# A two-layer transformer kernel: VectorE's score tile chosen further ahead, row sums laid over 128 partitions, LayerNorm without negated means, two memsets dropped

## The chip, the cores and the metric

The kernel runs on one core of one Trainium2 chip. The metric is device microseconds of one execution. A few executions are taken per kernel, and each version is timed in the same rounds and on the same chip as the kernel before. The experiments ran in four such sets of rounds on different chips, where the median of the kernel before lay between 1650.24 and 1652.71 us; a difference between versions of different sets is less sure by as much. Runs of a kernel mostly agree within about 0.3%; the widest spread of one set is 0.5%. The trace of each kernel is of one profiled execution.

The engines, as the profile names them: PE is TensorE (PEld its weight loads), DVE is VectorE, ACT is ScalarE, POOL is GpSimd, SP issues most DMAs.

## The reference

Two layers, each of attention and a gated feed-forward block, both behind a LayerNorm without weights. 2,048 tokens, width 512, 32 heads of 16, feed-forward width 1,792, bfloat16 inputs.

```python
def _layernorm(x, axis=-1, eps=1e-5):
    m = jnp.mean(x, axis=axis, keepdims=True)
    v = jnp.var(x, axis=axis, keepdims=True)
    return (x - m) / jnp.sqrt(v + eps)
# A: qkv, softmax(q k^T / 4) v, output projection; 32 heads of 16
# B: (gelu(x w_gate) * (x w_up)) w_down
x = A_x
x = x + A(_layernorm(x)); x = x + B(_layernorm(x))     # the same weights in both layers
x = x + A(_layernorm(x)); x = x + B(_layernorm(x))
```

## The kernel before

The program is recorded by a scheduler that runs at build time. Each instruction is given an assumed cost in microseconds (`cost`, `us`). The scheduler plays the engines forward in assumed time, and each engine's instruction order follows from that. On the chip the order is fixed: TensorE executes its matmuls in that order and stops at the first one whose semaphore, the signal that its operand is ready, has not come; a timeline below shows it stopped for 1.1 to 1.7 us.

A score tile is 128 keys by 512 queries for one head (two halves of 256 in the last block). A slot computes two or three tiles for ScalarE, which exponentiates them in one instruction (`PT<-PS`), and perhaps one more for VectorE. VectorE makes its exponential with integer arithmetic on the float16 bits (`PI<-PS`) and three shifted copies (`PP<-PI`). That costs four PV matmuls for the tile instead of one. VectorE's tile is chosen here:

```python
    def pick(look=False):
        cap = slot_cap()
        want_d = not look and started_all() and behind() < LAG and vector_tile()  # vector_tile: VectorE not late
        ...
        a, d = [], None
        for x in cur:
            if len(a) == cap and (d is not None or not want_d):
                break
            t = x[3]                                   # tile number; t % 4 is its row group
            if want_d and d is None and d_tile(x) and (not dg["items"] or dg["uk"] == x[:3]):
                if len(a) == cap or all(y[3] % 4 != t % 4 for y in a):
                    d = x
                    continue
            if len(a) < cap:
                a.append(x)
            elif x[3] > a[-1][3] + 3 or x[:3] != a[-1][:3]:
                break
        return a, d
```

LayerNorm is bn_stats on VectorE, three small GpSimd instructions, and one instruction per 128 rows that applies it ("the normalisation" below). That last one is on VectorE for the whole first LayerNorm, and in each later LayerNorm on GpSimd for three of the four blocks of 512 tokens and on VectorE for the last (abridged):

```python
    def ln_scale(n, then, lo=0):
        ...
        job("pool", 1, [
            (lambda e: e.tensor_scalar(LNS[:, 0, lo:lo + n], var, LN_EPS, None, op0=ALU.add), ..., 0.25),
            (lambda e: e.tensor_tensor(LNS[:, 1, lo:lo + n], LNS[:, 0, lo:lo + n], CM05[:, 0:n], op=ALU.pow), ..., 0.45 + 0.16 * n),
            (lambda e: e.tensor_scalar(LNS[:, 2, lo:lo + n], mean, -1.0, None, op0=ALU.mult), ..., 0.25)], then)

    def ln_apply(i, rows, key, eng, alt, then=None, us=None, st=0):
        us = us or (1.05 if eng == "pool" else 0.46)          # the assumed cost
        job(eng, 1, [(lambda e: e.tensor_scalar(xn(i, alt), rows, LNS[:, 2, st + i:st + i + 1], LNS[:, 1, st + i:st + i + 1],
                                                op0=ALU.add, op1=ALU.mult), ..., us)], then, ported=True)
```

TensorE then transposes the normalised rows (`HT`), and the projections of the feed-forward block or of the next layer follow. The row sums of the softmax are gathered by DMA into `LT` (16 partitions by 128 per head group, 8 in the half blocks), inverted there by VectorE, written to DRAM (`rscr`) and loaded, spread, into `RB`. GpSimd multiplies that into the attention output (`AT`). Where TensorE has nothing ready, the scheduler inserts filler matmuls (`ONB` by `ZV`), which are meant to keep its clock up.

Of the kernel before, what the change touches and what calls it, by code (L numbers as in the profile page):

```python
# [14 lines left out]
AP = bass.AP  # L15
# [160 lines left out]
def _emit_fast(nc, es, x_in, wqkv, wo, wg, wu, wd, out, n_rep=2):  # L176
# [193 lines left out]
    sch.op("pool", lambda e: e.memset(OKV[:], 1.0), w=[("OKV",)])  # L370
    sch.op("pool", lambda e: e.memset(AP(VP, 16, [[NKT * H * VW, 128], [VW, NKT * H]]), 1.0), w=[("VPONE",)], cost=0.9)
    sch.op("pool", lambda e: e.memset(OKL[:], 1.0), w=[("OKL",)], cost=0.2)
    sch.op("pool", lambda e: e.memset(LT[:], 1.0), w=[("LT", i) for i in range(NG)], cost=0.2)
    sch.op("pool", lambda e: e.memset(RB[:], 0.0), w=[("RB", i) for i in range(NRB)], cost=0.9)
    dma("sp", "ldw_o", WO[:], wo.rearrange("(a p) n -> p a n", p=128), w=[("WO",)], kb=512)


# [205 lines left out]

    def ln_scale(n, then, lo=0):
        keys = [("MV", lo + i) for i in range(n)]
        mean = AP(MV, 2 * lo, [[16, 128], [2, n]])
        var = AP(MV, 2 * lo + 1, [[16, 128], [2, n]])
        job("pool", 1, [
            (lambda e: e.tensor_scalar(LNS[:, 0, lo:lo + n], var, LN_EPS, None, op0=ALU.add), keys,
             [("LNS", lo + i) for i in range(n)], 0.25),  # L590
            (lambda e: e.tensor_tensor(LNS[:, 1, lo:lo + n], LNS[:, 0, lo:lo + n], CM05[:, 0:n], op=ALU.pow),
             [("LNS", lo + i) for i in range(n)] + [("CM05",)], [("LNS", lo + i) for i in range(n)], 0.45 + 0.16 * n),
            (lambda e: e.tensor_scalar(LNS[:, 2, lo:lo + n], mean, -1.0, None, op0=ALU.mult),
             keys + [("LNS", lo + i) for i in range(n)], [("LNS", lo + i) for i in range(n)], 0.25)], then)

    def ln_check(n, lo=0):
        var = AP(MV, 2 * lo + 1, [[16, 128], [2, n]])
# [2 lines left out]

    def ln_apply(i, rows, key, eng, alt, then=None, us=None, st=0):
        us = us or (1.05 if eng == "pool" else 0.46)
        job(eng, 1, [(lambda e: e.tensor_scalar(xn(i, alt), rows, LNS[:, 2, st + i:st + i + 1], LNS[:, 1, st + i:st + i + 1],
                                                op0=ALU.add, op1=ALU.mult),
                      [key, ("LNS", st + i)], [xnkey(i, alt)], us)], then, ported=True)

    def transpose_piece(i, tt, alt=False, eng="dve", then=None):
        def fn(e, bs):
# [244 lines left out]
    def normalise(layer, qb, gs, half, h):  # L853

        n = len(gs)
        lr = 16 if h is None else 8
        np_ = lr * n
        q0, qn = (0, 512) if h is None else (256 * h, 256)
        hs = (0, 1) if h is None else (h,)
        lk = [("LT", i) for i in range(n)]  # L860
        ops = [(lambda e: e.reciprocal(LT[0:np_, :], LT[0:np_, :]), lk, lk, 0.87)]
        final = h == 1 and gs[-1] == NG - 1
        go = move_act if final else move

        def then(o):
            there = []
            checks = []
            for lim, op in ((1.0 / L_LO, ALU.is_le), (1.0 / L_HI, ALU.is_ge)):
                checks.append((lambda e, lim=lim, op=op: e.scalar_tensor_tensor(
                    OKL[0:np_, :], LT[0:np_, :], lim, OKL[0:np_, :], op0=op, op1=ALU.mult),  # L870
                    lk + [("OKL",)], [("OKL",)], 0.31))
            dve(1, checks, got(("ok", layer, qb, h, gs[-1])))

            def stored(o, i):
                there.append(i)
                if len(there) == n:
                    lt["held"] = False
                    while lt["next"]:
                        lt["next"].pop(0)()
                g = gs[i]  # L880
                rs_here.add((layer, qb, h, g))
                if (layer, qb, h, g ^ 1) in rs_here:
                    pairs_q.append(((layer, qb * NG + (g | 1), h), lambda: spread(g & ~1)))
                    next_pair()

            for i in range(n):
                g = gs[i]
                go(0, "rs%d" % i, AP(RSC, (RC(qb, h, g) * 8 + g % 2) * 512, [[2 * 512, 4], [1, qn]]),
                   LT[lr * i:lr * i + lr, :], [("LT", i)], [("RSC", RC(qb, h, g), g % 2)],
                   lambda o, i=i: stored(o, i), kb=8)  # L890

        def spread(g):
            c = g // 2
            slot = rb_free.pop(0)
            here = []
            ds = [os_of.pop((layer, qb * NG + g + k, h)) for k in range(2)]
            assert g % 2 == 0 and ds[1] == ds[0] + 1

            def landed(o):
                here.append(o)  # L900
                if len(here) == 2:
                    job("pool", 1, [(lambda e: e.tensor_tensor(AT[:, c, q0:q0 + qn], OP[:, slot, 0:qn], RB[:, slot, 0:qn],  # L902
                                                               op=ALU.mult),
                                     [("OP", slot), ("RB", slot)], [("AT", c, k) for k in hs], 0.03 + 0.00258 * qn)],
                        done)

            def done(o):
                have.update(("norm", layer, qb, h, g + k) for k in range(2))
                rb_free.append(slot)
                next_pair()  # L910

            move(0, "op%d" % slot, OP[:, slot, 0:qn],
                 OSD[ds[0] // 2, :, 0:qn],
                 [("OSD", d, j) for d in ds for j in range(4)], [("OP", slot)], landed, kb=qn / 2)
            go(0, "rb%d" % slot, RB[:, slot, 0:qn],
               AP(RSC, RC(qb, h, g) * 8 * 512, [[512, 8], [0, 16], [1, qn]]),
               [("RSC", RC(qb, h, g), k) for k in range(2)], [("RB", slot)], landed, kb=qn / 2)

        dve(1, ops, then)
# [6 lines left out]
    def evac(layer, u, part):  # L926
# [13 lines left out]
        def then(o):  # L940
            acc["free"] = True
            if part == "A":
                return
            og = list(range(NG))
            sizes = [NG - 2, 1, 1] if h == 1 else [NG - 2, 2]
            pos = g
            k, lo = 0, 0
            while pos >= lo + sizes[k]:
                lo += sizes[k]
                k += 1  # L950
            i = pos - lo
            lr = 16 if h is None else 8
            units_done[layer] += 1
            bd = block_done[layer, qb, h] = block_done.get((layer, qb, h), 0) + 1

            gone = []

            def put(o):
                gone.append(o)
                if len(gone) == 4:  # L960
                    os_free.append(s)
                    stored_os.add((layer, u, h))
                    next_pair()
                    if h != 1 or g != NG - 1:
                        gathered(o)

            def put_out(o):
                for j in range(4):
                    move(0, "os%d_%d" % (s, j), OSD[d // 2, 32 * j + 16 * (d % 2):32 * j + 16 * (d % 2) + 16, 0:qn],
                         OS[32 * j:32 * j + 16, s, 0:qn], [("OS", s)], [("OSD", d, j)], put, kb=qn / 16)  # L970
                if h == 1 and g == NG - 1:
                    gathered(o)

            def gathered(o):
                if i == sizes[k] - 1:
                    lt["held"] = True
                    normalise(layer, qb, og[lo:lo + sizes[k]], k % 2, h)

            d = (layer * NU + u + (NG if h == 1 else 0)) % NOD
            os_of[layer, u, h] = d  # L980

            def gather():
                (move_act if h == 1 and g == NG - 1 else move)(0, "lt%d" % i, LT[lr * i:lr * i + lr, :],
                     AP(OS, 16 * NOS * 512 + s * 512, [[32 * NOS * 512, 4], [1, qn]]),
                     [("OS", s)], [("LT", i)], put_out)
            if lt["held"]:
                lt["next"].append(gather)
            else:
                gather()
            if bd == NG:  # L990
                posts.append(post(layer, qb, h))
# [262 lines left out]
    def pick(look=False):  # L1254
# [4 lines left out]
        if bd is None or sch.ready("pe", w=[BK[bd]]) > now[0] + 0.02:  # L1259
            want_d = False  # L1260
        a, d = [], None
        for x in cur:
            if len(a) == cap and (d is not None or not want_d):
                break
            t = x[3]
            if want_d and d is None and d_tile(x) and (not dg["items"] or dg["uk"] == x[:3]):
                if len(a) == cap or all(y[3] % 4 != t % 4 for y in a):
                    d = x
                    continue
            if len(a) < cap:  # L1270
                a.append(x)
            elif x[3] > a[-1][3] + 3 or x[:3] != a[-1][:3]:
                break
        return a, d

    def pull():
        while len(cur) < 6 and nxt[0] < len(segs):
# [1293 lines left out]
```

## Time and profile before

Before: 1653.57 us, the median of 3 runs (1649.52 to 1655.59).

The profile page of the kernel before: first the busy time of each engine, its share of the span and its number of instructions, then two lines of the chain that ended last, by engine and by line.

```profile
PE 1559.9 (95%) x16441; PEld 521.8 (32%) x16441; DVE 1362.6 (83%) x2336; ACT 1568.5 (95%) x1351; POOL 176.6 (11%) x233
...
ACT 60%; PE 31%; DVE 6%; DMA 1%; issue 1%; POOL 1%; SPq 0%; DVEq 0%; POOLq 0%
ACT fPT L1387 57%; PE fPS L1373 9%; PE fPS L1519 8%; PE fPS L1054 7%; PE fPS L633 3%; ACT fHT L1336 2%; PE fPS L1118 2%; DVE fPI L1427 2%; DVE fPP L1467 2%; PE fPS L1539 1%; DMA fRB<-rscr 1%; ACT L1336 1%; PE fPS L700 1%; DVE fHT L1073 0%; 
```

ScalarE is the engine to watch. The chain runs through its exponential for 57% of the span, the largest share of any line. TensorE's 95% contains filler, so its share alone says little.

Groups of instructions of the kernel before, shapes apart. A line gives source line, engine, operation, output<-input, shapes and count; then busy us, mean ns of one; then idle us of the engine just before them and who ended it. Records of exponentials overlap on ScalarE: the busy times of the two groups below add up to 1,672 us, and together they cover only 1,492.5.

```profile
L1387 ACT ACTIVATE fPT<-fPS 128x1536 bf16<-128x1536 f32 x652 | 972.5, 1492 | 27.2 <-PE fPS L1373 24.4
L1387 ACT ACTIVATE fPT<-fPS 128x1024 bf16<-128x1024 f32 x655 | 699.5, 1068 | 6.5 <-PE fPS L1373 5.5
...
L603 POOL TENSOR_SCALAR fHT<-fX,fLNS 128x512 f16<-128x512 f32 x36 | 29.1, 814 | 2.1 <-PE fPS L1373 0.4 <-POOL fLNS L593 0.2
...
L593 POOL TENSOR_SCALAR fLNS<-fMV 128x2 f32<-128x2 f32 x25 | 8.1, 326 | 2.3
...
L861 DVE RECIPROCAL fLT<-fLT 96x128 f32<-96x128 f32 x7 | 6.6, 940 | 0.0
...
L603 DVE TENSOR_SCALAR fHT<-fX,fLNS 128x512 f16<-128x512 f32 x12 | 6.1, 535 | 1.8 <-POOL fLNS L593 1.8
...
L861 DVE RECIPROCAL fLT<-fLT 8x128 f32<-8x128 f32 x2 | 1.9, 936 | 0.6 <-DMA fLT<-fOS 0.6
```

Of 4,096 score tiles, 830 go to VectorE and the others to 1,307 exponentials. ScalarE is idle for 27.2 + 6.5 = 33.7 us before exponentials in all. A reciprocal takes 0.94 us, whether for 96 partitions or 8.

Who waited for whom, kernel before: us in total, times, longest us.

```profile
ACT fPT L1387 <- PE fPS L1373: 29.9, 62, 3.7
...
PE fPS L610 <- POOL fHT L603: 0.5, 1, 0.5
```

TensorE waits almost never for GpSimd's normalised rows: once, 0.5 us.

### The profile page before, as it was taken

The page shows a single profiled execution, that of the slowest core. Times are in us where ns is not written, and L with a number is a line of the kernel's source. Part 1 is how long each engine was busy: PE and PEld are TensorE (multiplying, and loading weights), DVE is VectorE, ACT ScalarE, POOL GpSimd, SP SyncE. Part 2 cuts the span into 40 slices and gives each one's busy share as a digit, 9 for nine tenths or more (in the row PEclk, how much of TensorE's full clock was granted, in tenths as well). Part 3 has the DMA queues.
Part 4 walks back from the last instruction along what each step waited for, and adds up shares of the span by engine and source line. Part 5 has one row for each costly group of instructions (what it writes and reads, how often), then busy time and mean ns, then how long its engine had stood idle before and what let it go on. Part 6 is the DMA issues. An engine that isn't in the chain of part 4 may idle for free.

```text
span 1650.3 us, 38750 instructions
## 1 busy us (share of the span) xinstructions
PE 1559.9 (95%) x16441; PEld 521.8 (32%) x16441; DVE 1362.6 (83%) x2336; ACT 1568.5 (95%) x1351; POOL 176.6 (11%) x233
## 2 busy tenths in 40 slices
PE   8999899999999999999999989999999998999998
PEld 3332222222222223332333322222222222444455
DVE  7989998879988899887743999988898879888773
ACT  6999999999999999999999999999999999899981
POOL 3420010002100210002410110100010000100000
PEclk9999999999999999999999999999999999999999
DMA  5200101123011321113123010220401123022234
GB/s 147 59 8 8 45 22 52 43 75 96 21 53 36 105 56 28 56 33 110 44 65 120 12 55 19 59 58 24 124 21 48 48 63 88 20 65 61 74 117 118
DMA packets 120962, 97.22 MB, mean 59 GB/s; under 512 B 11472, under 2 KB 103888, under 8 KB 120784
## 3 DMA queue, kind: packets, MB, share of 16 engines
q1 hardware_dynamic: 116928, 89.95, 19.1%
q0 software_dynamic: 2112, 4.19, 1.0%
q8 instruction: 133, 2.18, 0.6%
q10 hardware_dynamic: 1744, 0.53, 0.1%
q14 instruction: 45, 0.37, 0.1%
HBM read 76.81 MB, written 15.20 MB: 56 GB/s over the span
## 4 chain that ended last, share of the span: by engine, by line
ACT 60%; PE 31%; DVE 6%; DMA 1%; issue 1%; POOL 1%; SPq 0%; DVEq 0%; POOLq 0%
ACT fPT L1387 57%; PE fPS L1373 9%; PE fPS L1519 8%; PE fPS L1054 7%; PE fPS L633 3%; ACT fHT L1336 2%; PE fPS L1118 2%; DVE fPI L1427 2%; DVE fPP L1467 2%; PE fPS L1539 1%; DMA fRB<-rscr 1%; ACT L1336 1%; PE fPS L700 1%; DVE fHT L1073 0%; ACT L1387 0%
## 5 line engine op out<-in xcount | busy, mean ns | idle before, releaser
L1387 ACT ACTIVATE fPT<-fPS 128x1536 bf16<-128x1536 f32 (+1 forms) x1307 | 1492.5, 1279 | 33.7 <-PE fPS L1373 29.9
L1427 DVE TENSOR_SCALAR fPI<-fPS 128x512 int16<-128x512 f32 x830 | 564.1, 684 | 111.3 <-PE fPS L1373 105.6
L1373 PE MATMUL fPS<-fQ,fKT 32*128 32x512 f16 (+1 forms) x4608 | 528.7, 359 | 57.5 <-ACT fPT L1387 43.2
L1519 PE MATMUL fPS<-fPT,fVP 128*17 128x512 bf16 (+1 forms) x3676 | 463.1, 359 | 8.2 <-DVE fOS L937 3.8
L1467 DVE TENSOR_SCALAR fPP<-fPI 128x2048 int16<-128x2048 int16 (+3 forms) x705 | 427.0, 636 | 11.8 <-PE fPS L1519 5.6
L1519 PE MATMUL fPS<-fPP,fVD 128*17 128x512 f16 (+1 forms) x2796 | 394.1, 359 | 2.2 <-POOL fVD L713 0.9
L1373 PEld LDWEIGHTS fPS<-fQ,fKT 32*128 32x128 f16 x4608 | 142.8, 91 | 535.2 <-ACT fPT L1387 385.0
L1519 PE MATMUL fPS<-fPI,fVP 128*17 128x512 f16 (+1 forms) x932 | 256.1, 359 | 1.7 <-DVE fOS L937 1.0
L1054 PE MATMUL fPS<-fXNT,fWR 128*128 128x512 f16 (+1 forms) x952 | 219.5, 362 | 6.3 <-DVE fHT L1097 4.6
L1519 PEld LDWEIGHTS fPS<-fPT,fVP 128*17 128x17 f16 x3676 | 117.9, 88 | 151.3 <-issue 89.9
L902 POOL TENSOR_TENSOR fAT<-fOP,fRB 128x512 f16<-128x512 f32 (+1 forms) x36 | 43.7, 1214 | 1124.2 <-DMA fRB<-rscr 1124.2
L1539 PE MATMUL fPS<-fONB,fZV 128*17 128x512 f16 x1804 | 143.3, 387 | 1.7 <-POOL fQMASK L364 1.5
L1519 PEld LDWEIGHTS fPS<-fPP,fVD 128*17 128x17 f16 x2796 | 107.0, 89 | 103.4 <-issue 48.5
L1118 PE MATMUL fPS<-fWR,fHT 128*128 128x512 bf16 x428 | 118.2, 383 | 0.5 <-DVE fQ L679 0.3
L1054 PEld LDWEIGHTS fPS<-fXNT,fWR 128*128 128x128 bf16 x952 | 77.0, 97 | 111.8 <-issue 21.6
L1097 DVE TENSOR_TENSOR fHT<-fPS,fHT 128x512 bf16<-128x512 f32 x112 | 76.4, 688 | 42.5 <-PE fPS L1054 32.0
L1073 DVE CAST fHT<-fPS 128x512 bf16<-128x512 f32 x105 | 71.6, 686 | 29.4 <-PE fPS L1054 29.3
L1519 PEld LDWEIGHTS fPS<-fPI,fVP 128*17 128x17 f16 x932 | 64.0, 88 | 36.1 <-issue 19.0
L713 POOL TENSOR_SCALAR fVD<-fVP 128x544 f16<-128x544 f16 (+1 forms) x48 | 54.1, 1129 | 110.5 <-DVE fVP L721 107.8
L1539 PEld LDWEIGHTS fPS<-fONB,fZV 128*17 128x17 f16 x1804 | 42.1, 91 | 47.8 <-issue 24.4
L937 DVE COPY fOS<-fPS 128x512 f32<-128x512 f32 (+1 forms) x72 | 45.0, 625 | 13.7 <-PE fPS L1519 13.3
L679 DVE TENSOR_SCALAR fQ<-fPS,fQMASK 128x512 f16<-128x512 f32 (+1 forms) x72 | 46.1, 681 | 6.1 <-PE fPS L633 6.1
(71 smaller groups left out, 657.4 us busy)
## 6 DMA issues: line engine op xcount, KB each, us to landing
fWR<-in_B_w_up_dram SPq DMA_DIRECT2D x62, 256.0 KB, 2.9
fWR<-in_B_w_down_dram SPq DMA_DIRECT2D x58, 256.0 KB, 2.8
fWR<-in_B_w_gate_dram SPq DMA_DIRECT2D x57, 256.0 KB, 5.1
oscr<-fOS SPq DMA_DIRECT2D x224, 32.0 KB, 1.7
fOP<-oscr SPq DMA_DIRECT2D x28, 256.0 KB, 2.7
fRB<-rscr SPq DMA_DIRECT2D x28, 256.0 KB
fX<-in_A_x_dram POOLq DMA_DIRECT2D x4, 1024.0 KB, 5.8
xscr<-fX SPq DMA_DIRECT2D x16, 256.0 KB, 2.9
```

The lines of the kernel that those rows point to most:

```text
L633: ins = e.matmul(bank(bs[0])[:, 0:cols], lhsT=l, rhs=r_, start=(i == 0), stop=(i == n - 1))
L713: job("pool", 2, [(lambda e, dst=dst, src=src, ph=ph: e.tensor_scalar(dst, src, 2.0 ** (-ph / NPH), None, op0=ALU.mult), [("VP", c, k) for ...
L1054: ins = e.matmul(bank(bs[0])[:, w * qn:(w + 1) * qn], lhsT=wchunk(s, (ft + w) % 2, ck), rhs=XNT[:, ck, xs], start=(ck == 0), stop=(ck == N ...
L1073: evac_job(1, b, [(lambda e: e.tensor_copy(in_ht(ft), in_bank(b)), [BK[b]], fk, 0.6)], got(("gate", layer, qb, h, ft)))
L1097: (lambda e: e.tensor_tensor(in_ht(ft), in_bank(b), in_ht(ft), op=ALU.mult), [BK[b]] + fk, fk, 0.62)], got(("up", layer, qb, h, ft))))
L1118: ins = e.matmul(bank(b)[:, 0:D], lhsT=HT[:, ft, i * 128:(i + 1) * 128], rhs=wslot(s)[:, jj * D:(jj + 1) * D], start=(ft == 0), stop=(ft = ...
L1373: ins = e.matmul(bank(b)[:, b0:b0 + qn], lhsT=KT[32 * j:32 * j + 32, (x[1] % NG) // 2, kt * 128:(kt + 1) * 128], rhs=Q[32 * j:32 * j + 32, ...
L1387: o = sch.op("act", lambda e: e.activation(PT[:, p, 0:512 * na].rearrange("p (a b) -> p a b", a=na), PS[:, b0:b0 + na, :], ACTF.Exp, scale ...
L1427: dve(0, [(lambda e: e.tensor_scalar(PI[:, gi, 512 * r:512 * (r + 1)], bank(bd), DBIAS, 0.0, op0=ALU.add, op1=ALU.max), [BK[bd]], [("PI", ...
L1467: shifts.append((s, [(lambda e: e.tensor_scalar(PP[:, s, 0:512 * n], PI[:, gi, 0:512 * n], int(OCT) * ph // NPH, None, op0=ALU.add), [("PI ...
L1519: ins = e.matmul(PS[32 * j:32 * j + VW, ACC, 0:qn], lhsT=l, rhs=r_, start=a, stop=z, tile_position=(0, 32 * j), skip_group_check=True)
L1539: ins = e.matmul(PS[32 * j:32 * j + VW, ACC, :], lhsT=ZV[:, :], rhs=ones, start=False, stop=False, tile_position=(0, 32 * j), skip_group_c ...
```

## The change

The intent: choose VectorE's tile so that its 32-row group of the array is free and its matmul runs beside the others; invert the row sums with all 128 partitions, so that a reciprocal has 96 columns or fewer; drop the negated mean, a GpSimd instruction, by subtracting the mean directly; drop two memsets that are no longer needed.

```diff
-    sch.op("pool", lambda e: e.memset(LT[:], 1.0), w=[("LT", i) for i in range(NG)], cost=0.2)
-    sch.op("pool", lambda e: e.memset(RB[:], 0.0), w=[("RB", i) for i in range(NRB)], cost=0.9)
 ... in ln_scale
-            (lambda e: e.tensor_scalar(LNS[:, 2, lo:lo + n], mean, -1.0, None, op0=ALU.mult), ...
 ... in ln_apply
-        job(eng, 1, [(lambda e: e.tensor_scalar(xn(i, alt), rows, LNS[:, 2, st + i:st + i + 1], LNS[:, 1, st + i:st + i + 1],
-                                                op0=ALU.add, op1=ALU.mult),
+        job(eng, 1, [(lambda e: e.tensor_scalar(xn(i, alt), rows, MV[:, st + i, 0:1], LNS[:, 1, st + i:st + i + 1],
+                                                op0=ALU.subtract, op1=ALU.mult),
 ... in normalise; the DMAs to and from LT and the two checks likewise
-        ops = [(lambda e: e.reciprocal(LT[0:np_, :], LT[0:np_, :]), lk, lk, 0.87)]
+        ops = [(lambda e: e.reciprocal(LT[:, 0:nw], LT[:, 0:nw]), lk, lk, 0.07 + 0.0068 * nw)]
 ... in pick
-        for x in cur:
-            if len(a) == cap and (d is not None or not want_d):
+        spare = None
+        for k, x in enumerate(cur):
+            if len(a) == cap and (d is not None or not want_d or k >= 12):
                 break
...
-                if len(a) == cap or all(y[3] % 4 != t % 4 for y in a):
+                if all(y[3] % 4 != t % 4 for y in a):
                     d = x
                     continue
+                if len(a) == cap and spare is None:
+                    spare = x
             if len(a) < cap:
                 a.append(x)
-            elif x[3] > a[-1][3] + 3 or x[:3] != a[-1][:3]:
+            elif not want_d:
                 break
-        return a, d
+        return a, d if d is not None else spare
```

More of the change, by code (lines that the diff above doesn't have):

```diff
@@ L585, in ln_scale @@
         keys = [("MV", lo + i) for i in range(n)]
-        mean = AP(MV, 2 * lo, [[16, 128], [2, n]])
         var = AP(MV, 2 * lo + 1, [[16, 128], [2, n]])
@@ L591, in ln_scale @@
             (lambda e: e.tensor_tensor(LNS[:, 1, lo:lo + n], LNS[:, 0, lo:lo + n], CM05[:, 0:n], op=ALU.pow),
-             [("LNS", lo + i) for i in range(n)] + [("CM05",)], [("LNS", lo + i) for i in range(n)], 0.45 + 0.16 * n),
-            (lambda e: e.tensor_scalar(LNS[:, 2, lo:lo + n], mean, -1.0, None, op0=ALU.mult),
-             keys + [("LNS", lo + i) for i in range(n)], [("LNS", lo + i) for i in range(n)], 0.25)], then)
+             [("LNS", lo + i) for i in range(n)] + [("CM05",)], [("LNS", lo + i) for i in range(n)], 0.45 + 0.16 * n)], then)
     def ln_check(n, lo=0):
@@ L602, in ln_apply @@
         us = us or (1.05 if eng == "pool" else 0.46)
-        job(eng, 1, [(lambda e: e.tensor_scalar(xn(i, alt), rows, LNS[:, 2, st + i:st + i + 1], LNS[:, 1, st + i:st + i + 1],
-                                                op0=ALU.add, op1=ALU.mult),
-                      [key, ("LNS", st + i)], [xnkey(i, alt)], us)], then, ported=True)
+        job(eng, 1, [(lambda e: e.tensor_scalar(xn(i, alt), rows, MV[:, st + i, 0:1], LNS[:, 1, st + i:st + i + 1],
+                                                op0=ALU.subtract, op1=ALU.mult),
+                      [key, ("LNS", st + i), ("MV", st + i)], [xnkey(i, alt)], us)], then, ported=True)
     def transpose_piece(i, tt, alt=False, eng="dve", then=None):
@@ L855, in normalise @@
         n = len(gs)
-        lr = 16 if h is None else 8
-        np_ = lr * n
+        w = 4 * (512 if h is None else 256) // 128
+        nw = w * n
         q0, qn = (0, 512) if h is None else (256 * h, 256)
@@ L869, in then @@
                 checks.append((lambda e, lim=lim, op=op: e.scalar_tensor_tensor(
-                    OKL[0:np_, :], LT[0:np_, :], lim, OKL[0:np_, :], op0=op, op1=ALU.mult),
-                    lk + [("OKL",)], [("OKL",)], 0.31))
+                    OKL[:, 0:nw], LT[:, 0:nw], lim, OKL[:, 0:nw], op0=op, op1=ALU.mult),
+                    lk + [("OKL",)], [("OKL",)], 0.08 + 0.0018 * nw))
             dve(1, checks, got(("ok", layer, qb, h, gs[-1])))
@@ L888, in then @@
                 go(0, "rs%d" % i, AP(RSC, (RC(qb, h, g) * 8 + g % 2) * 512, [[2 * 512, 4], [1, qn]]),
-                   LT[lr * i:lr * i + lr, :], [("LT", i)], [("RSC", RC(qb, h, g), g % 2)],
+                   LT[:, w * i:w * i + w], [("LT", i)], [("RSC", RC(qb, h, g), g % 2)],
                    lambda o, i=i: stored(o, i), kb=8)
@@ L951, in then @@
             i = pos - lo
-            lr = 16 if h is None else 8
+            w = 4 * qn // 128
             units_done[layer] += 1
@@ L982, in gather @@
             def gather():
-                (move_act if h == 1 and g == NG - 1 else move)(0, "lt%d" % i, LT[lr * i:lr * i + lr, :],
+                (move_act if h == 1 and g == NG - 1 else move)(0, "lt%d" % i, LT[:, w * i:w * i + w],
                      AP(OS, 16 * NOS * 512 + s * 512, [[32 * NOS * 512, 4], [1, qn]]),
```

## The prediction

> **What bounds it.** ScalarE. The page's busy table gives ScalarE 95%, VectorE 83%; TensorE's 95% contains 1,804 filler matmuls (143 us). The chain that ended last is 57% the exponential (PT<-PS). In long runs of the timeline one exponential issues every 1.14 us (60 in 68.25 us). Between the first (14.85 us) and the last (1605.4 us), 1,307 exponentials account for about 1,487 us, GELU 47, table loads 21, and 34 us are idle before exponentials, 29.9 of them for score matmuls (the table of waits). Before lie 15 us of head, after it 45 us of tail.
>
> **What changes** (from the built instruction orders).
> 1. Tile choice. Of 4,096 score tiles VectorE takes 845 instead of 830; exponentials fall to 1,301 (three of 1536 and three of 1024 columns fewer): 6 x 1.14 = 6.8 us less on the bounding chain. VectorE gains 15 x 0.68 us plus shifts (24 more of 2048 at 0.70, 15 fewer of 1536 at 0.56, 6 fewer of 512), about 17 us, in an engine with 288 us idle. TensorE gains 60 PV matmuls net, four abreast, about 3 us.
> 2. Row groups. Slots whose tiles share a row group fall from 93 to 69. A score group without such a clash takes 0.39 us in the trace, with one 0.60 us: 24 x 0.21 = 5 us of TensorE, which cancels the added PV work. The Trainium skill ("TensorE: Matmul & The Clock Gate", Part 3) says that K=32 matmuls in different row groups run concurrently; this trace agrees (three within 0.39 us). It counts only where TensorE is late: I credit 2 us of the 29.9.
> 3. Row sums over 128 partitions. Reciprocals take 0.93-0.94 us whatever the partitions (8 to 96, by 128 columns). Scaled by columns, an estimate, 96 columns take 0.7, 32 take 0.3, 8 take 0.13 us: 8 us of VectorE, and 4 more over the checks; off the critical path except in the tail (-0.8). Against it each gather and write-back has 128 runs of 32 or 64 bytes instead of 8 or 16 of 512 ("DMA: Bandwidth & Descriptors", the box on SBUF tile shape: the shape sets the descriptor count). This trace has almost no such packets; from 18 ns for one of 256 bytes I estimate 0.2 to 0.4 us more per transfer, so the chain to RB is about even.
> 4. LayerNorm: 30 GpSimd instructions of 0.23-0.33 us gone; 0.3 us at the head, 0.2 in the tail.
> 5. Memsets (0.22 and 0.54 us): mostly swallowed by VectorE's wait for input rows.
>
> **Sum.** -6.8 - 2 - 0.4 (head) - 0.3 (tail), about -9.5 us; rearranging costs some waits, so I take off 1 us: **1645 us**, 80% range 1636 to 1653. Chances: faster by over 2% 0.01, within 2% 0.98, slower 0.01.
>
> **What would show it.** Exponential busy down by 7 to 8 us (1,492.5 to about 1,485) at the same mean; idle before exponentials 28 to 34 us; score groups of 0.6 us rarer; reciprocals of 0.13 to 0.75 us; first exponential at about 14.5 us, last about 9 us earlier; tail 45 us within 1 us.
>
> **What would make it wrong.** The order is fixed at build time from assumed durations. If the small-run transfers take over 1 us longer, AT comes late, TensorE stalls in order and its clock drops (as once at 1,407 us, 2 us), and 2 to 5 us per block boundary are lost (8 of them). Conversely, if many of the 43 us that score matmuls wait for ScalarE stem from clashes, the gain could reach 15 us.

## The result, and the profile after

After: 1660.31 us median of 4 runs (1659.58 to 1662.31), against 1652.55 us for the kernel before in the same rounds (4 runs). The ratio is 1.0049, 95% interval 1.0027 to 1.007. Ratios here are the mean time of one kernel's fast runs over that of the other's of the same rounds, so not quite the ratio of the medians quoted. The change made the kernel about 8 us slower, clear of noise. The predicted 1645 us, with a range of 1636 to 1653, was wrong, and in its direction too.

The page of the kernel after, the same lines:

```profile
PE 1561.2 (94%) x16477; PEld 517.8 (31%) x16477; DVE 1368.1 (82%) x2354; ACT 1566.4 (94%) x1345; POOL 220.5 (13%) x201
...
ACT 47%; PE 35%; DVE 9%; POOL 5%; DMA 3%; issue 1%; SPq 0%; DVEq 0%; POOLq 0%; ACTq 0%
ACT fPT L1385 44%; PE fPS L1517 10%; PE fPS L1371 10%; PE fPS L1049 7%; PE fPS L1113 3%; DVE fPI L1425 3%; POOL fHT L598 3%; DVE fPP L1465 3%; PE fPS L628 3%; ACT fHT L1334 2%; DMA fRB<-rscr 2%; PE fPS L1537 1%; POOL fLNS L588 1%; ACT L1334
```

The chain is less ScalarE's than before (44% in the exponential instead of 57%), and GpSimd, which had 1%, has 5% of it. Its busy time rose from 176.6 to 220.5 us, although 32 instructions left it.

The same groups of the kernel after, in the order of its profile (the negated means are gone):

```profile
L1385 ACT ACTIVATE fPT<-fPS 128x1536 bf16<-128x1536 f32 x649 | 967.9, 1491 | 38.5 <-PE fPS L1371 34.6
L1385 ACT ACTIVATE fPT<-fPS 128x1024 bf16<-128x1024 f32 x652 | 695.8, 1067 | 8.9 <-PE fPS L1371 7.8
...
L598 POOL TENSOR_SCALAR fHT<-fX,fMV,fLNS 128x512 f16<-128x512 f32 x36 | 82.4, 2296 | 2.9 <-PE fPS L1113 1.0 <-POOL fLNS L588 0.2
...
L598 DVE TENSOR_SCALAR fHT<-fX,fMV,fLNS 128x512 f16<-128x512 f32 x12 | 6.6, 587 | 0.7 <-POOL fLNS L588 0.7
...
L856 DVE RECIPROCAL fLT<-fLT 128x96 f32<-128x96 f32 x7 | 5.2, 743 | 0.1
...
L856 DVE RECIPROCAL fLT<-fLT 128x8 f32<-128x8 f32 x2 | 0.4, 203 | 0.7 <-DMA fLT<-fOS 0.7
```

The exponentials did become fewer: 649 + 652 = 1,301. But ScalarE's idle time before them grew from 33.7 to 38.5 + 8.9 = 47.4 us. One line stands out: the GpSimd normalisation, with as many elements as before, takes 2.30 us in the mean (median 2.08) instead of 0.81. VectorE's, with the same new operators, did not change its pace: 0.59 us against 0.54 for float32 rows, and 0.40 both times for bfloat16 rows.

Who waited for whom, kernel after:

```profile
ACT fPT L1385 <- PE fPS L1371: 42.4, 82, 4.0
...
PE fPS L605 <- POOL fHT L598: 14.9, 16, 1.9
```

TensorE now waits 16 times for GpSimd's normalised rows, 14.9 us in all. ScalarE waits for score matmuls 12.5 us longer than before. At one block boundary this is easy to follow in the timeline of the kernel after (start us, duration us, engine, line, instruction; in brackets the idle time before it). First GpSimd, two normalisations per line:

```profile
575.95 5.09 POOL L598 TENSOR_SCALAR fHT<-fX,fMV,fLNS 128x512 f16<-128x512 f32 x2
...
582.15 5.02 POOL L598 TENSOR_SCALAR fHT<-fX,fMV,fLNS 128x512 f16<-128x512 f32 x2
```

Then TensorE, whose transposes wait for those rows:

```profile
581.19 0.38 PE L605 MATMUL fPS<-fIDN,fHT 128*128 128x128 f16 x4 [1.42 <-POOL fHT L598]
...
585.25 0.38 PE L605 MATMUL fPS<-fIDN,fHT 128*128 128x128 f16 x4 [1.14 <-POOL fHT L598]
...
587.32 0.58 PE L605 MATMUL fPS<-fIDN,fHT 128*128 128x128 f16 x4 [1.68 <-POOL fHT L598]
```

Then ScalarE in the same stretch:

```profile
583.14 2.37 ACT L1385 ACTIVATE fPT<-fPS 128x1536 bf16<-128x1536 f32 x2 [2.14 <-PE fPS L1371]
588.49 2.36 ACT L1385 ACTIVATE fPT<-fPS 128x1536 bf16<-128x1536 f32 x2 [2.98 <-PE fPS L1371]
```

Three transposes stand 1.1 to 1.7 us each for GpSimd, and the score matmuls queue behind them. ScalarE then has nothing to exponentiate for 2.1 and 3.0 us. The clock that TensorE was granted falls too. The stretch of 550 to 600 us: busy us and number of instructions of PE, PEld, DVE, ACT and POOL, then the clock (here 0.93), the DMA share and GB/s.

```profile
550.00:600.00 50.00, 43.84 (x422) 12.33 (x423) 39.09 (x67) 43.66 (x39) 16.53 (x12) 0.93 0.41 113
```

Over the whole run the clock is 0.993, against 0.999 before. Between 50 and 1,600 us it is below 1.00 in seven stretches of 50 us (0.93 to 0.99) here, and in one (0.97) before. Taken by these shares, an estimate, the lower clock cost TensorE 10 us of full speed here and 1.5 before. So part of the loss came by way of the clock; how much was not separated from the waits themselves.

Where the time went, from the profiled runs: "head" ends with the start of the first exponential, "tail" begins with the end of the last.

| kernel | head us | body us | tail us | exponentials |
|---|---|---|---|---|
| before | 14.9 | 1590.6 | 44.9 | 1,307 |
| after | 13.9 | 1601.9 | 44.3 | 1,301 |

The loss is all in the body, where six exponentials fewer should have saved time.

### The profile page after: what moved, and what is told of

The parts are those of the page before. It is cut to its first block, busy times and chain, and to the rows that moved or that the text cites. A ratio compares the mean times of both kernels' runs of the same rounds, so it can differ in the third digit from the quotient of the medians.

```text
span 1660.1 us, 38796 instructions
## 1 busy us (share of the span) xinstructions
PE 1561.2 (94%) x16477; PEld 517.8 (31%) x16477; DVE 1368.1 (82%) x2354; ACT 1566.4 (94%) x1345; POOL 220.5 (13%) x201
## 4 chain that ended last, share of the span: by engine, by line
ACT 47%; PE 35%; DVE 9%; POOL 5%; DMA 3%; issue 1%; SPq 0%; DVEq 0%; POOLq 0%; ACTq 0%
ACT fPT L1385 44%; PE fPS L1517 10%; PE fPS L1371 10%; PE fPS L1049 7%; PE fPS L1113 3%; DVE fPI L1425 3%; POOL fHT L598 3%; DVE fPP L1465 3%; PE fPS L628 3%; ACT fHT L1334 2%; DMA fRB<-rscr 2%; PE fPS L1537 1%; POOL fLNS L588 1%; ACT L1334 1%; DMA rscr<-fLT 1%
## 5 line engine op out<-in xcount | busy, mean ns | idle before, releaser
L1385 ACT ACTIVATE fPT<-fPS 128x1536 bf16<-128x1536 f32 (+1 forms) x1301 | 1490.5, 1279 | 47.5 <-PE fPS L1371 42.4
L1425 DVE TENSOR_SCALAR fPI<-fPS 128x512 int16<-128x512 f32 x845 | 573.9, 685 | 103.6 <-PE fPS L1371 98.0
L1517 PE MATMUL fPS<-fPT,fVP 128*17 128x512 bf16 (+1 forms) x3656 | 472.0, 360 | 6.9 <-DVE fOS L932 2.8
L1465 DVE TENSOR_SCALAR fPP<-fPI 128x2048 int16<-128x2048 int16 (+3 forms) x708 | 436.6, 645 | 10.7 <-PE fPS L1517 4.6
L1517 PE MATMUL fPS<-fPP,fVD 128*17 128x512 f16 (+1 forms) x2856 | 415.7, 358 | 2.9 <-POOL fVD L708 1.0
L1517 PEld LDWEIGHTS fPS<-fPP,fVD 128*17 128x17 f16 x2856 | 111.1, 89 | 105.2 <-issue 51.8
L598 POOL TENSOR_SCALAR fHT<-fX,fMV,fLNS 128x512 f16<-128x512 f32 x36 | 82.4, 2296 | 2.9 <-PE fPS L1113 1.0
```

Of the source, the lines that this page charges most:

```text
L598: job(eng, 1, [(lambda e: e.tensor_scalar(xn(i, alt), rows, MV[:, st + i, 0:1], LNS[:, 1, st + i:st + i + 1], op0=ALU.subtract, op1=ALU.mult),
L1385: o = sch.op("act", lambda e: e.activation(PT[:, p, 0:512 * na].rearrange("p (a b) -> p a b", a=na), PS[:, b0:b0 + na, :], ACTF.Exp, scale ...
L1425: dve(0, [(lambda e: e.tensor_scalar(PI[:, gi, 512 * r:512 * (r + 1)], bank(bd), DBIAS, 0.0, op0=ALU.add, op1=ALU.max), [BK[bd]], [("PI", ...
L1465: shifts.append((s, [(lambda e: e.tensor_scalar(PP[:, s, 0:512 * n], PI[:, gi, 0:512 * n], int(OCT) * ph // NPH, None, op0=ALU.add), [("PI ...
L1517: ins = e.matmul(PS[32 * j:32 * j + VW, ACC, 0:qn], lhsT=l, rhs=r_, start=a, stop=z, tile_position=(0, 32 * j), skip_group_check=True)
```

## The experiments

The theory: the GpSimd normalisation with subtract and multiply takes 2.08 us where add and multiply took 0.77. The fixed order assumed 1.05 us, so transposes come up too early and hold the score matmuls behind them. The rivals: the new tile choice itself makes waits; the transfers with short runs make the attention output late; the place of the operand (mean read from `MV` beside `LNS`) makes the instruction slow, not its operator; or the slow instruction hurts by itself, however it is ordered.

### The change with the old LayerNorm

```diff
 the kernel after, with ln_scale and ln_apply of the kernel before
```

Expected:

> Theory (the GpSimd normalisation with subtract takes 2.08 us instead of 0.77, and the fixed order assumed 1.05): with the old LayerNorm (negated mean, add then multiply) and all other parts of the change, the GpSimd normalisation is back at 0.77 us, the transposes' wait for it falls from 14.9 to under 2 us, and the time is 1640 to 1648 us. Rival (the reordered tile choice itself costs waits): 1655 to 1662 us.

Measured: 1642.05 us (1641.26 to 1643.26, 4 runs) against 1652.71 for before; ratio 0.9932 (0.9915 to 0.9949); correct. GpSimd's normalisation is back at 0.88 us in the mean, and TensorE's table of waits has no wait of transposes for it. The LayerNorm part alone turns a gain of 0.7% into a loss of 0.5%. The tile choice does not cost 10 us.

### Only the LayerNorm part, on the kernel before

```diff
 the kernel before, with ln_scale and ln_apply of the kernel after
```

Expected:

> Only the LayerNorm part on the kernel before. Theory: GpSimd normalisation 2.08 us, transposes wait about 15 us for it, and the time is 1660 to 1672 us, 8 to 18 us slower than before. Rival (tile choice is the cost): 1650 to 1655 us, as before.

Measured: 1666.34 us (1665.53 to 1668.08); ratio 1.0084 (1.0067 to 1.0101); correct. GpSimd's normalisation takes 2.20 us in the mean, and transposes wait for it 20 times, 16.3 us in all:

```profile
PE fPS L607 <- POOL fHT L600: 16.3, 20, 1.7
```

The part costs some 14 us without the tile choice or the row sums. In the profiled run 8.2 us of it are in the body, where the clock is below 1.00 in three stretches only (0.97 to 0.99): the waits cost time without much help of the clock. The rest is in the head (1.4 us) and in the tail (3.7 us), where 236 filler matmuls instead of 160 end 2.6 us after the last projection's operand was ready.

### Only the tile choice, on the kernel before

```diff
 the kernel before, with pick of the kernel after
```

Expected:

> Only the tile choice on the kernel before. Theory: 1642 to 1648 us, some 7 us faster than before, with fewer exponentials. Rival (tile choice is the cost): 1658 us or more.

Measured: 1655.62 us (1651.04 to 1656.86); ratio 1.0008 (0.9985 to 1.003); correct. Neither the theory nor the rival had this: the choice alone does nothing to the time, though it has 1,304 exponentials, three fewer. In the profiled run the body is 3.5 us shorter (1587.0) and the tail 5.3 us longer (50.2). The tail is looked into further down.

### One operator of the kernel after changed

```diff
-                                                op0=ALU.subtract, op1=ALU.mult),
+                                                op0=ALU.add, op1=ALU.mult),
```

Expected:

> The kernel after with one operator changed in the normalisation, add for subtract, the mean still read from MV: a wrong result on purpose, but the same instructions in the same order as after. Theory: the operator is the cause, so 0.77 us per GpSimd normalisation and 1640 to 1648 us. Rival (the operand's place, two scalars from different tiles, is the cause): still 2.08 us and 1660 us.

Measured: 1644.00 us (1643.47 to 1644.26); ratio 0.9945 (0.9929 to 0.9962); the result is wrong (relative error 0.65). The orders of all five engines are those of the kernel after, row for row; only the 36 normalisations of GpSimd and the 28 of VectorE differ, in their operator. GpSimd's group of this run:

```profile
L598 POOL TENSOR_SCALAR fHT<-fX,fMV,fLNS 128x512 f16<-128x512 f32 x36 | 29.2, 819 | 3.2 <-PE fPS L1113 1.4 <-POOL fLNS L588 0.2
```

With the same operands in the same places, GpSimd is back at 0.82 us. The operand's place is ruled out. The one operator is worth 1660.31 - 1644.00 = 16.3 us (the two were timed in different rounds, against 1652.55 and 1652.71 us for the kernel before). VectorE's 0.59 us for float32 rows is found here too, with add, so it does not come from the operator. At the boundary shown above, this run's GpSimd line and TensorE's transposes read as follows:

```profile
571.42 1.52 POOL L598 TENSOR_SCALAR fHT<-fX,fMV,fLNS 128x512 f16<-128x512 f32 x2
...
575.21 1.51 POOL L598 TENSOR_SCALAR fHT<-fX,fMV,fLNS 128x512 f16<-128x512 f32 x2
```

```profile
573.98 0.40 PE L605 MATMUL fPS<-fIDN,fHT 128*128 128x128 f16 x4
...
575.16 0.40 PE L605 MATMUL fPS<-fIDN,fHT 128*128 128x128 f16 x4
...
579.75 0.91 PE L605 MATMUL fPS<-fIDN,fHT 128*128 128x128 f16 x8
```

None of these transposes waits, and the clock of the stretch is 1.00:

```profile
550.00:600.00 50.00, 46.08 (x479) 13.60 (x478) 45.21 (x77) 47.72 (x43) 10.91 (x12) 1.00 0.47 115
```

It is 1.00 in every other stretch of the body, too.

### The same slow instruction, but the order made for it

```diff
-        us = us or (1.05 if eng == "pool" else 0.46)
+        us = us or (2.3 if eng == "pool" else 0.46)
```

Expected:

> The kernel after with the GpSimd normalisation's assumed cost raised from 1.05 to 2.3 us, so that the order is made for the slow instruction. Theory (it is the late arrival in a fixed order that costs, not the GpSimd time itself): the transposes' wait for GpSimd falls from 14.9 us to under 4, time 1642 to 1650 us, GpSimd normalisation still at 2.08 us. Rival (the slow instruction costs by itself, by delaying the feed-forward block): 1655 us or more.

Measured: 1647.71 us (1646.5 to 1649.71) against 1651.94 for before; ratio 0.9978 (0.9962 to 0.9995); correct. GpSimd's group of this run:

```profile
L598 POOL TENSOR_SCALAR fHT<-fX,fMV,fLNS 128x512 f16<-128x512 f32 x36 | 80.7, 2250 | 8.8 <-PE fPS L1113 7.1 <-POOL fLNS L588 0.2
```

GpSimd is as slow as in the kernel after, yet no wait of transposes for it is left in TensorE's table of waits. The longest that is left for normalised rows is for VectorE's:

```profile
PE fPS L605 <- DVE fHT L598: 1.9, 2, 1.5
```

And 1660.31 - 1647.71 = 12.6 of the 16.3 us are back (again from different rounds). So the lateness in a fixed order, with the lower clock that went with it, was the larger part of the cost. A slow instruction on an engine that is idle for 87% of the time cost less than 4 us here (1647.71 against 1644.00) once the order knew of it.

### Only the row sums over 128 partitions, on the kernel before

```diff
 the kernel before, with LT's layout, the reciprocal and its assumed cost, and the checks of the kernel after
```

Expected:

> Only the row sums over 128 partitions on the kernel before. The scheduler then places 1,303 exponentials, four fewer than before, and 200 fillers ahead of the last output projection instead of 160. Theory (this part is worth the exponentials, its transfers cost 0.1 to 0.3 us each, the tail pays for the fillers): 1645 to 1651 us. Rival (small transfers hurt): over 1655 us.

Measured: 1645.94 us (1645.57 to 1646.56); ratio 0.9966 (0.995 to 0.9983); correct. In the profiled run the body is 1582.1 us, 8.5 us shorter. This part has 1,303 exponentials, four fewer than before, without the new tile choice. The reason lies in the assumed costs. `vector_tile` gives VectorE a tile only when its assumed backlog is short, and the assumed reciprocals and checks became shorter. A build without a run confirms it for the order: the kernel before with only these two assumed costs changed, and the old layout of `LT`, has the same 1,303 exponentials and the same order on every engine. How much of the 6 us comes from that order, and how much from the reciprocals being shorter on the chip, no run isolates.

### GpSimd adds a negated mean, VectorE subtracts

```diff
+            ([] if eng == "dve" else [ the negated mean, as before ])
-                                                op0=ALU.subtract, op1=ALU.mult),
+                 op0=ALU.subtract if eng == "dve" else ALU.add, op1=ALU.mult),   # operand likewise
```

Expected:

> The kernel after, but the GpSimd normalisation adds a negated mean as before, while VectorE's subtracts the mean directly. All GpSimd normalisations back at 0.77 us, transposes' wait under 3 us; 164 fillers ahead of the last projection against 140 in the kernel after. Theory: 1640 to 1648 us, correct, as fast as the change with the old LayerNorm (1642).

Measured: 1644.95 us (1643.37 to 1646.91); ratio 0.9956 (0.9939 to 0.9972); correct. It is as expected, and its interval overlaps that of the version with the whole old LayerNorm: no gain is shown from dropping the negated mean at head and tail.

### Every normalisation on VectorE

```diff
-        ..., "dve" if qb == NQB - 1 else "pool", ...
+        ..., "dve", ...
```

Expected:

> The kernel after with every normalisation on VectorE, subtract kept: VectorE showed no difference between the operators (0.41 us before and after). Theory: no GpSimd normalisation is left, 36 more on VectorE at about 0.55 us, 20 us in an engine with 290 us idle; the order is right again, so 1640 to 1650 us. Rival (subtract is slow on VectorE too for float32 rows, or VectorE is too full): above 1655 us.

Measured: 1649.16 us (1646.2 to 1651.11) against 1650.24; ratio 0.9987 (0.997 to 1.0003); correct. All 48 normalisations of float32 rows take 0.55 us in the mean, so the slow operator is GpSimd's alone. The median is inside the expected range, but the gain over before is not shown: the body is 1589.2 us, against 1583.7 with the operator mended. Why VectorE gives back what GpSimd loses was not tested. The trace shows two exponentials more (1,303), 4.4 us of TensorE's waits for `AT` instead of 1.2, and one stretch with a clock of 0.97.

### The tile choice with fewer fillers in the tail

```diff
+        if not left() and "wo" not in have and log.get("tail", 0) >= 35:    # no more than 35 groups of four
+            now[0] = t + 0.05
+            continue
```

Expected:

> Only the tile choice on the kernel before, with the filler matmuls ahead of the last output projection cut from 264 to 140; every other TensorE row is unchanged. Theory (those fillers held the projection 4.3 us past its operand and hid what the tile choice gains): the projection starts within 1 us of its operand and the time is 1650 to 1653 us, some 4 us below the 1655.6 of the uncapped kernel. Rival (the choice itself gains nothing): 1655 us as before the cap.

TensorE in the tail with the tile choice alone; `AT` was ready 4.3 us before the projection (WO by AT) could start:

```profile
1609.10 14.42 PE L1542 MATMUL fPS<-fONB,fZV 128*17 128x512 f16 x264
1623.46 1.90 PE L633 MATMUL fPS<-fWO,fAT 128*128 128x512 bf16 x8
```

And with the cap:

```profile
1607.76 7.73 PE L1544 MATMUL fPS<-fONB,fZV 128*17 128x512 f16 x140
1618.41 3.39 PE L633 MATMUL fPS<-fWO,fAT 128*128 128x512 bf16 x8 [2.92 <-POOL fAT L902]
```

The uncapped order has 264 fillers there (the kernel before has 160, the kernel after 140). The projection started at 1623.46 us, where GpSimd had finished its operand at 1619.13. With the cap it starts 0.05 us after its operand, but the eight matmuls then take 3.39 instead of 1.90 us, after 2.9 us of idle TensorE: the granted clock of these 3.39 us is 0.55, and 1.00 in the uncapped run. So in this trace 1.5 us were lost again where the fillers were gone and the clock fell. The tail is 47.5 us, 2.7 shorter. The median, 1650.93 us (1650.24 to 1652.01; ratio 0.9994, 0.9977 to 1.0011), is 4.7 us below that of the uncapped kernel, but taken in other rounds, and the two ratios' intervals overlap. So the trace shows the fillers' delay; the size of the gain in time is inconclusive. So is the gain of the tile choice by itself: its body is 3.7 us shorter than before, and its time, in the same rounds, is the same.

### GpSimd operators side by side

```diff
+    for rep in range(2):      # after the last instruction of the kernel before, 128 x 512 float32 each
+        e.tensor_scalar(o, X[:, 0, :], s0, s1, op0=ALU.add, op1=ALU.mult)        # and twelve other forms
```

Expected:

> The kernel before with 13 GpSimd instructions on 128 by 512 float32 appended, twice over, to time operators side by side: tensor_scalar add-mult, subtract-mult, mult-add, mult-subtract, add alone, subtract alone, subtract-mult with constants, subtract-mult to float32, max-mult, mult-mult, add-add, and tensor_tensor add and subtract. Theory (the operator pair decides): add-mult 0.77 us, subtract-mult 2.08 us whatever the scalars' place and the output type; no expectation for the others. The run's time means nothing.

Nine of the thirteen groups, in the order of the profile. In the order of the lines below: subtract-mult; add-add; mult-subtract; max-mult; add alone; subtract alone; tensor_tensor add; mult-add; add-mult.

```profile
L1721 POOL TENSOR_SCALAR fAT<-fX,fLNS 128x512 f16<-128x512 f32 x2 | 4.2, 2116 | 0.2
L1730 POOL TENSOR_SCALAR fAT<-fX,fLNS 128x512 f16<-128x512 f32 x2 | 4.2, 2094 | 0.2
L1723 POOL TENSOR_SCALAR fAT<-fX,fLNS 128x512 f16<-128x512 f32 x2 | 4.2, 2092 | 0.2
L1728 POOL TENSOR_SCALAR fAT<-fX,fLNS 128x512 f16<-128x512 f32 x2 | 4.2, 2076 | 0.0
...
L1724 POOL TENSOR_SCALAR fAT<-fX,fLNS 128x512 f16<-128x512 f32 x2 | 3.1, 1575 | 0.2
L1725 POOL TENSOR_SCALAR fAT<-fX,fLNS 128x512 f16<-128x512 f32 x2 | 3.1, 1564 | 0.2
...
L1731 POOL TENSOR_TENSOR fRB<-fX 128x512 f32<-128x512 f32 x2 | 2.5, 1268 | 0.0
...
L1722 POOL TENSOR_SCALAR fAT<-fX,fLNS 128x512 f16<-128x512 f32 x2 | 1.5, 772 | 0.2
L1720 POOL TENSOR_SCALAR fAT<-fX,fLNS 128x512 f16<-128x512 f32 x2 | 1.5, 772 | 0.0
```

Not shown: subtract-mult with a float32 output 2.07 us, with constants for scalars 1.93 (2.08 was expected); mult-mult 0.77; tensor_tensor subtract 1.26. So it is no matter of subtraction as such. Three pairs run at 0.77 us: add-mult, mult-add and mult-mult. All other forms of tensor_scalar that were tried take 1.6 to 2.1 us, also an addition alone, which does less. The Trainium skill ("GPSIMD Engine Reference", section 3.1) predicts 768 ns for 512 elements in its best case, a tight loop without branches that depend on the data. Our fast pairs agree at 772 to 774 ns, and the page says nothing of operator pairs that miss it by a factor of 2.7. Why these three are fast was not tested.

### A lone multiply made a pair

```diff
-                        dst, src, 2.0 ** (-ph / NPH), None, op0=ALU.mult)
+                        dst, src, 2.0 ** (-ph / NPH), 1.0, op0=ALU.mult, op1=ALU.mult)
```

This is the version with the old LayerNorm, whose 48 GpSimd scalings of V are a lone multiply. It was run in five rounds beside the same kernel without this edit.

Expected:

> The change with the old LayerNorm, and the 48 GpSimd scalings of V written as multiply, multiply by 1.0 instead of a lone multiply; the order of all engines is the same, instruction for instruction. If the operators timed side by side carry over, a scaling of 544 columns falls from 1.62 to about 0.8 us and one of 136 from 0.66 to about 0.45 us. As GpSimd is hardly waited for there (1 to 3 us in all), the time falls by 0 to 2 us against the same kernel without it: 1640 to 1643 us.

Expected of its neighbour:

> The change with the old LayerNorm once more, unchanged, in the rounds of the kernel above, for the comparison and as a repeat: 1641 to 1644 us.

GpSimd's scalings of 544 columns, without the edit:

```profile
L711 POOL TENSOR_SCALAR fVD<-fVP 128x544 f16<-128x544 f16 x24 | 38.8, 1616 | 78.4 <-DVE fVP L719 77.1
```

With it:

```profile
L711 POOL TENSOR_SCALAR fVD<-fVP 128x544 f16<-128x544 f16 x24 | 16.2, 676 | 86.1 <-DVE fVP L719 84.8
```

Doing one multiplication more makes the instruction 2.4 times faster, and the scalings of 136 columns went from 0.66 to 0.36 us. Both are faster than was expected (0.8 and 0.45). So for a lone multiply and mult-mult the finding carries over to float16 and other widths. The times are 1641.12 us (1639.51 to 1642.79, ratio 0.9932) with it and 1641.56 us (1639.04 to 1642.96, ratio 0.9935) without it, 6 runs each: no difference, as GpSimd is hardly waited for there. These are the fastest versions found, both about 0.7% under the kernel before, and both correct. They also show more than the row sums alone gave (ratio 0.9966): the tile choice and the two dropped memsets, on top of the row sums, seem to be worth 0.3% more, though the tile choice alone gained nothing. The intervals touch, the rounds were others, and no run tells the two parts apart.

### All in one table

Ratios are to the kernel before in the same rounds. Head, body and tail are of the profiled run.

| kernel | median us | ratio | GpSimd normalisation, mean us | head / body / tail us |
|---|---|---|---|---|
| after | 1660.31 | 1.0049 | 2.30 | 13.9 / 1601.9 / 44.3 |
| after, old LayerNorm | 1642.05 | 0.9932 | 0.88 | 14.9 / 1581.2 / 45.4 |
| before, new LayerNorm | 1666.34 | 1.0084 | 2.20 | 16.3 / 1598.8 / 48.6 |
| before, new tile choice | 1655.62 | 1.0008 | 0.85 | 17.1 / 1587.0 / 50.2 |
| the same, tail capped | 1650.93 | 0.9994 | 0.86 | 15.9 / 1586.9 / 47.5 |
| before, new row sums | 1645.94 | 0.9966 | 0.84 | 15.2 / 1582.1 / 45.6 |
| after, add for subtract (wrong result) | 1644.00 | 0.9945 | 0.82 | 14.3 / 1583.7 / 43.6 |
| after, assumed cost 2.3 us | 1647.71 | 0.9978 | 2.25 | 15.1 / 1585.5 / 44.4 |
| after, GpSimd adds, VectorE subtracts | 1644.95 | 0.9956 | 0.85 | 15.0 / 1585.0 / 45.1 |
| after, all on VectorE | 1649.16 | 0.9987 | none | 15.2 / 1589.2 / 44.9 |
| after, old LayerNorm, again | 1641.56 | 0.9935 | 0.88 | 13.8 / 1580.0 / 45.6 |
| the same, multiply made a pair | 1641.12 | 0.9932 | 0.87 | 15.3 / 1580.3 / 45.4 |

One thing in these times is not in the traces. The time of a run is longer than its profiled span, by 3.2 to 3.7 us for the kernel before and by 1.7 to 3.0 us for every other version. So up to about 2 us of each version's advantage over the kernel before lies outside the span, and nobody looked for the reason. By spans alone the tile choice is 4.5 us longer than the kernel before in the median (0.7 with the tail capped), and the version with every normalisation on VectorE 0.5 us. The kernel after and the run with its operator changed have the same 2.2 us, so the 16.3 us between them stand.

## Why the prediction was wrong

The step that failed is point 4, "LayerNorm: 30 GpSimd instructions of 0.23-0.33 us gone; 0.3 us at the head, 0.2 in the tail". It counted the instructions that left and took the one that changed, from add-mult to subtract-mult, to cost the same. On GpSimd it went from 0.77 to 2.08 us in the median. With its consequences in the fixed order, waits of the transposes and a lower clock, that cost 16.3 us by the medians, measured by the run that changes only this operator and keeps every engine's order. Without it the time is 1644.0 us, against 1645 predicted. That the sum holds so well is partly luck: its largest term, the 6.8 us of the tile choice, was put on the wrong part, as follows.

The other points, one by one:

- "What bounds it" held: with the operator mended, the body of the profiled run shrinks by 6.9 us (1590.6 to 1583.7), and the sum had 7.8 us there (6.8 and 2, less 1).
- The tile choice was not worth what point 1 gave it. The six exponentials fewer are right as a count, but the row sums alone have four fewer and 6.0 us less time, and the tile choice alone three fewer and no gain in time. On top of the row sums it may be worth some 4 to 5 us, with the memsets (above). The prediction put the whole gain on the tile choice because it read only the two complete orders; the parts were not ordered one by one.
- Point 2, fewer clashes of row groups: the built orders say 93 and 69 slots. In the traces, groups of back-to-back score matmuls (no gap above 0.15 us) that last 0.55 to 0.75 us fall from 108 to 102, to 90 with the operator mended, where the clock stays up, and to 87 with the tile choice alone. The direction is right. What it is worth in time is not isolated; it is within what the tile choice alone gained, which was nothing measurable.
- Point 3: the reciprocals went as estimated (0.74, 0.34 and 0.20 us for 96, 32 and 8 columns, where 0.7, 0.3 and 0.13 were said). The chain to `RB` is about even, too: but for the last block, the first load of `RB` after a write-back was issued 1.35 or 1.85 us after it, and 1.27 or 2.0 us in the kernel after. That this part lies "off the critical path except in the tail" was wrong in its effect: alone it gained 6.0 us, with an order that the scheduler changed because of it.
- Point 5 and the head: the first exponential starts at 13.9 us, 14.5 was predicted. But it varies from 13.8 to 17.1 us between the profiled runs, and from 13.8 to 14.9 between two of the same kernel (after, old LayerNorm), so nothing can be read from it. The tail of 44.3 us is within the 1 us predicted.
- "Exponential busy down by 7 to 8 us" was a bad sign to name: it fell by 2.0 us only (1,492.5 to 1,490.5), as the records overlap and the sum of their union grows where ScalarE waits between them. The count and the idle time before them say more.
- "What would make it wrong" had the mechanism, and the wrong trigger: an operand comes late, TensorE stalls in order, its clock drops. `AT` was not late (TensorE waited 1.4 us for it, 2.7 before); the normalised rows in `HT` were (14.9 us, 0.5 before).

## What to carry to other kernels

A changed operator in an otherwise equal instruction is a new cost: measure it on the engine it runs on before it goes into a schedule, since VectorE's indifference to subtract or add said nothing about GpSimd's. Where a fixed order is made from assumed durations, compare each duration in the trace with its assumption after every change; an instruction on an engine with 87% idle time cost 1% of the run, mostly because each of them took 1 us longer than assumed (2.08 against 1.05). On GpSimd, a tensor_scalar form that was fast in a trace (here add-mult, mult-add, mult-mult, at 0.77 us against 1.6 to 2.1) is worth keeping where the engine is waited for, even at the price of a negated operand; a multiplication by one made an instruction shorter here, but not the kernel.

## What the Trainium skill lacked or had wrong

- "GPSIMD Engine Reference" (section 3.1) gives a best case of 768 ns for 512 elements, and does not say that the time depends on the operator pair. Here add-mult, mult-add and mult-mult take 0.77 us on 128 by 512 float32; subtract-mult, mult-subtract, max-mult and add-add 2.08 to 2.12; add or subtract alone 1.56 to 1.58.
- The same page (section 4.1) calls one-input work on GpSimd "roughly line-rate". A lone multiply of 128 by 544 float16 took 1.62 us, and with a second multiplication by 1.0 it took 0.68.
- "DMA: Bandwidth & Descriptors", in its box on the SBUF tile shape, leaves open, for a load from flat DRAM, whether a tile of one row or one over 128 partitions is faster. A nearby case here, small gathers from SBUF to SBUF, shows no clear difference: from the last gather's issue to the reciprocal in the tail 1.77 us in the kernel before, with 8 rows of 512 bytes, and 1.93 in the kernel after, with 128 of 32. Over all the traces of versions it is 1.8 to 2.8 and 1.9 to 3.1 us.
- Nothing wrong was found in "TensorE: Matmul & The Clock Gate" (Part 3), on matmuls in different row groups running side by side: three score matmuls in different row groups end within 0.39 us, and a group in which two share one lasts 0.60 us.
